# Block 0 of a convolution and two-layer kernel: its first layer from 12-bit operands, its staged words kept in g, five roundings of w_out moved behind it

## The chip, the cores and the metric

The kernel runs on one core of a Trainium2 chip. The metric is the time of one execution on the device, in microseconds, taken as the median of several runs. A core has TensorE (PE in the profile, with its weight loads as PEld), VectorE (DVE), ScalarE (ACT), GpSimd (POOL) and SyncE (SP), which issues most DMAs. Each engine works through its own queue of instructions in the order in which the program has them; semaphores join the queues.

## The reference

Eight sequences of 4096 tokens with 192 features go through a causal convolution of 7 taps, whose weights are a softmax shared by the 24 features of a head; then each token goes through two layers with a hard swish between them.

```python
w = softmax(weight)                         # 8 heads x 7 taps
out[b, s] = sum_k w[:, k] * x_pad[b, s + k]  # per head, 24 features each
h = x @ w_in                                # (32768, 192) @ (192, 2048)
g = h * clip(h + 3, 0, 6) / 6
return g @ w_out                            # (32768, 2048) @ (2048, 192)
```

w_in and w_out arrive as 64-bit floats. x, and the result, are 32-bit.

## The kernel before

Tokens are taken in 32 blocks of 1024, each block as two groups of 512 that lie in the two halves of the partitions. Features lie as 64 partitions by three thirds (K3 = 3). w_in's 2048 columns are 16 chunks of 128; a chunk index c runs from 0 to 7 and covers two of them, one for each half of the partitions. A first-layer unit (c, group) gives two PSUM banks: the group "own" multiplies y as it lies, the group "other" multiplies y with its two halves exchanged by DMA (`swap`). `relu` on ScalarE (L308) and `gate` on VectorE (L312) turn a unit's banks into its place in the tile g, which holds all of a block's hidden layer.

Blocks 1 to 31 use `first_layer` (L508): each operand is split into a high part of 12 bits (ScalarE multiplies by CUT and rounds, `high_of`, L480), a low part (the subtraction `low_of`, L483) and the full value. Three passes, high × high, low × high and full × low, are 18 matmuls for each unit, and PSUM is used as four slots of two banks. Their second layer (L593) is written out with due times. Block 0 is different: its first layer (`h_mm`, `half_mm`, L302) multiplies 32-bit operands, and its second layer `out_direct` (L347) runs three rounds over the eight chunks of w_out, four results side by side. w_out's chunk p is needed when a round comes to p.

The weights have no loading phase. Each of 16 units (eight of w_in, eight of w_out) goes through class `Rounding`, from 64-bit words to 32-bit floats: `load` (DMA on SP's queue, four units ahead), `split` (two instructions on VectorE, L177 and L181), `clamp` (three on ScalarE, L189, L192, L195), `join` (two on VectorE, L198 and L202, then a multiplication on POOL, L206). The order of all this is written by hand (`manual_schedule`): at the start the units 0 to 2 stand between the steps of block 0's convolution, of which TensorE takes one third (`pe_tap`, L794) after three matmuls on zeros (L802). In the loop over the 16 parts, ten of them (`slots`) carry the join of unit n, the clamp of n+1 and the split of n+2; three joins stand behind the loop.

```python
            def between():
                if more:
                    join(n)
                    clamp(n + 1)
            ...
            h_out(c, group, bs, (lambda: None) if first else between)
            if more:
                split(n + 2)
```

`prepare`, in the first round of `out_direct`, makes w_in's three parts for the later blocks from the finished w_in (`w_parts`: ScalarE L480 and L487, POOL L483), then block 1's convolution (L899) and its split. `begin_block_two`, in the third round, forms sums of w_out (L218, L565) and begins the next convolution.

Of the kernel before, what the change touches and what calls it, by code (L numbers as in the profile page):

```python
# [31 lines left out]
def kernel(  # L32
# [39 lines left out]
    start_pools, first_in = ExitStack(), ExitStack()  # L72
    stg = start_pools.enter_context(tc.tile_pool(name="stg", bufs=8))
    cnv = start_pools.enter_context(tc.tile_pool(name="cnv", bufs=4))
    fi = first_in.enter_context(tc.tile_pool(name="fi", bufs=1, side="right"))
# [40 lines left out]
    zeros = cnv.tile([P, N], F32, name="zeros", bufs=1)  # L116
    nc.vector.memset(zeros[:], 0.0)


    w_in = fi.tile([P, NP, K3, P], F32, name="w_in")  # L120


# [10 lines left out]
    def stage():  # L133
        return stg.tile([P, WS, 2], U32, name="stage")

    def load_w_in(j):
        st = stage()
        for half in range(2):
            nc.sync.dma_start(  # L139
                out=st[half * D2 : (half + 1) * D2].rearrange("p (s f) w -> p s (f w)", s=K3),  # L140
                in_=w_in_bits[j + half * NP].rearrange("p s f w -> p s (f w)"),
            )
        return st

    def load_w_out(j):
        st = stage()
        nc.sync.dma_start(
            out=st[:].rearrange("p (k d) w -> p k (d w)", k=2), in_=w_out_bits[:, j]
        )
        return st  # L150
# [7 lines left out]
    class Rounding:  # L158
# [13 lines left out]
        def split(self):  # L172
# [4 lines left out]
            nc.vector.tensor_scalar(  # L177
# [3 lines left out]
            nc.vector.tensor_scalar(  # L181
# [15 lines left out]
        def join(self):  # L197
            nc.vector.scalar_tensor_tensor(  # L198
                out=self.scale[:], in0=self.st[:, :, 1], scalar=0x80000000,
                in1=self.scale[:], op0=ALU.bitwise_and, op1=ALU.bitwise_or,  # L200
            )
            nc.vector.scalar_tensor_tensor(  # L202
                out=self.sig[:], in0=self.top[:], scalar=2.0**-20, in1=self.sig[:],
                op0=ALU.mult, op1=ALU.add,
            )
            nc.gpsimd.tensor_tensor(  # L206
                out=self.dst, in0=self.sig[:], in1=self.scale[:].bitcast(F32), op=ALU.mult
            )
    def w_in_unit(j):
        return Rounding(lambda: load_w_in(j), w_in[:, j].rearrange("p s f -> p (s f)"))  # L210

    def w_out_unit(j):
        dst = w_out[:, j, B11 : B22 + 1].rearrange("p b d -> p (b d)")
        return Rounding(lambda: load_w_out(j), dst)
# [29 lines left out]
    y_swapped = fi.tile([P, K3, N], F32, name="y_swapped")  # L244
    OWN, OTHER = 0, K3
# [29 lines left out]
    def swap_first(part):  # L275
        swap(y_swapped[:, part], y[:, part])

    g = cst.tile([P, NP, 2, G, N], F32, name="g")
# [6 lines left out]
    free_banks = list(range(2 * 4))  # L285

    def take():
        return free_banks.pop(0)

    def give(b):  # L290
        free_banks.append(b)

    def half_mm(k, b, w, third_of_y, start=False, stop=False, onto=False):

        r = slice(k * D2, (k + 1) * D2)  # L300
        src = y[r, third_of_y] if third_of_y < K3 else y_swapped[r, third_of_y - K3]
        nc.tensor.matmul(  # L302
            out=psum[:, b], lhsT=w[r], rhs=src, start=start, stop=stop,
            skip_group_check=onto,
        )
# [9 lines left out]

    def h_mm(c, group, bs, s, order=range(K3)):

        for k in range(2):
            half_mm(k, bs[k], w_in[:, c, s], group + s, s == order[0], s == order[-1])

    def g_of(c, group, k):

        return g[:, c, k, k if group == OWN else 1 - k]

    def h_out(c, group, bs, between):
        for k, b in enumerate(bs):
            relu(g_of(c, group, k), psum[:, b])
        between()
        for k, b in enumerate(bs):
            gate(g_of(c, group, k), psum[:, b])  # L330
            give(b)

# [44 lines left out]
    def out_direct(i, work):  # L383

        parts = [(k, q) for k in range(G) for q in range(G * NQ)]
        for r in range(0, len(parts), 4):
            b = take()
# [16 lines left out]
            give(b)  # L404
# [20 lines left out]

    def product(bank, j, n, q, ks=every, **tokens):
        x, w = prod[n]
        return mm(bank, j, S3 if n == 7 else x, w, q, ks, True, True, **tokens)

    def four(*parts):  # L430

        b = take()
        bank = psum[:, b]
        side_by_side(*[product(bank, j, n, q) for j, (n, q) in enumerate(parts)])
        return b, bank

    def three(n, n4, q4):
        return four(*[(n, q) for q in range(NQ)], (n4, q4))

    def by_quarters(n, q):  # L440

        b = take()
        bank = psum[:, b]
        w = NP // 4
        side_by_side(
            *[product(bank, j, n, q, range(j * w, (j + 1) * w)) for j in range(4)]
        )
        return b, bank
# [27 lines left out]
    def r32(ap):  # L476
        return ap.bitcast(F32R)

# [6 lines left out]
    def w_parts(high, low, full, w):  # L485
        high_of(high, w)
        nc.scalar.copy(out=r32(full), in_=w)  # L487
        low_of(low, w, high, nc.gpsimd)

    free_slots = list(range(4))  # L490
    y_own, y_other, pools, s1 = [], [None], [], []

    def swap_parts():
        y_other[0] = pools[0].tile([P, 2, K3, N], F32, name="y_other", tag="other")
        for n in range(2):
            swap(y_other[0][:, n], y_own[n])


    def first_layer(i, jobs):

        def unit(n):
            group, c = divmod(n, NP)
            slot = free_slots.pop(0)
            for m_, (wn, yn) in enumerate(PASSES):
                for s in range(K3):
                    for k in range(2):
                        r = slice(k * D2, (k + 1) * D2)
                        nc.tensor.matmul(  # L508
                            out=psum[:, 2 * slot + k], lhsT=r32(w_in_parts[wn][r, c, s]),
                            rhs=r32(y_other[0][r, yn, s] if group else y_own[yn][r, s]),  # L510
                            start=m_ == s == 0, stop=m_ == 2 and s == K3 - 1,
                            skip_group_check=True,
                        )
            both = psum[:, 2 * slot : 2 * slot + 2]
            to = g4[:, c, 1:3] if group else g4[:, c, 0::3]
# [263 lines left out]
    with tc.manual_schedule():  # L779
# [19 lines left out]
        b = take()  # L799
        for _ in range(3):  # L800

            nc.tensor.matmul(  # L802
                out=psum[:, b], lhsT=zeros[:, 0:P], rhs=zeros[:], start=True, stop=True
            )
        for k in range(KC):
# [3 lines left out]
        b1 = take()  # L809
        pe_tap(b1, 1, pe_taps, pe_taps)  # L810


        order = (pe_third, 0, 1)
        parts = [(c, group) for p in range(0, NP, 2) for group in (OWN, OTHER)
                 for c in (p, p + 1)]
        early = {}

        def begin(c, group):
            early[c, group] = take(), take()
            for s in order[:2]:  # L820
                h_mm(c, group, early[c, group], s, order)
# [3 lines left out]
        for k, u in enumerate(conv0[: per + 2 * pe_taps]):  # L825
# [3 lines left out]
            elif k == per - 3:  # L829
                join(0, more=False)  # L830
                split(1)
                nc.scalar.copy(out=y[:, pe_third], in_=psum[:, b])
                give(b)
                swap_first(thirds[pe_third])
                clamp(1)
            elif k in (per, per + 1):
                if k == per:
                    swap_first(thirds[0])
                    load(AHEAD)
                    begin(0, OWN)  # L840
# [8 lines left out]
        give(b1)  # L849
        swap_first(thirds[1])  # L850
# [5 lines left out]
        for c, group in ((0, OTHER), (1, OWN), (1, OTHER)):  # L856
            begin(c, group)
        for c, group in parts[: len(early)]:
            h_mm(c, group, early[c, group], order[2], order)

        slots = [0, 1, 3, 4, 6, 7, 9, 10, 12, 13]
        n = 3
        for slot, (c, group) in enumerate(parts):
            first = slot < len(early)
            if first:
                bs = early[c, group]
            else:
                bs = take(), take()
                for s in range(K3):
                    h_mm(c, group, bs, s)  # L870
            more = slot in slots

            def between():
# [3 lines left out]

            if slot == 6:
                x_tiles[1] = load_x(1)
            h_out(c, group, bs, (lambda: None) if first else between)  # L880
            if more:
                split(n + 2)
                if first:
                    between()
                n += 1
# [6 lines left out]
        late = ctx.enter_context(tc.tile_pool(name="late", bufs=1, reuse_waits="tile"))  # L892
        w_in_parts = [late.tile([P, NP, K3, P], F32, name=f"w_in{n}") for n in range(3)]
# [21 lines left out]
        def prepare():  # L915
            for n in range(0, NP, 4):
                r = slice(n, n + 4)
                w_parts(*[w[:, r] for w in w_in_parts], w_in[:, r])
            for job in conv_jobs(1):
                job()  # L920
            first_in.close()
            later = ctx.enter_context(tc.tile_pool(name="later", bufs=1, reuse_waits="tile"))
            y_own.extend(later.tile([P, K3, N], F32, name=f"y{n}") for n in range(2))
            pools.append(ctx.enter_context(tc.tile_pool(name="oth", bufs=1, reuse_waits="tile")))
# [69 lines left out]
```

## Time and profile before

| | |
|---|---|
| median of 3 runs | 2225.67 us (2225.53 to 2225.78) |
| the profiled execution | 2225.73 us, its span 2223.6 us |
| TensorE's share of the span | 100% (weight loads 69%) |
| VectorE, ScalarE, GpSimd | 81%, 42%, 37% |
| block 0's first layer, from and to | 17.3 to 58.5 us |
| block 0's second layer | 58.5 to 99.8 us |
| block 1's first layer | 99.9 to 132.7 us |

Times within the span are counted from its start. Each row of the timeline gives start, length, engine, line, operation, the tiles out and in, their shapes and how many instructions were merged. Instructions of one engine overlap a little, so the distance of two starts is shorter than the first one's length. The span ends about 2.1 us short of the measured time. A matmul of 32-bit operands shows as two records, one from 12-bit operands as one. Line numbers before the change are those of the kernel above; after it, `relu` is L299, `gate` L303, block 0's and all other first-layer matmuls L436 and `out_direct` L314.

### The profile page before, as it was taken

The numbers are of one execution on the slowest core, as the hardware profiler recorded it, in microseconds if no ns is written. First come the engines' busy times: TensorE is split into PE (matmuls) and PEld (weight loads), VectorE is DVE, ScalarE is ACT, GpSimd is POOL, SyncE is SP. The second block draws the span as 40 slices with busy tenths as digits, with TensorE's granted clock in tenths as the row PEclk, the third lists the DMA queues.
The fourth block names the chain that finished last, engine by engine and source line by source line (L and its number), as shares of the span: only waits on it lengthen the run. The fifth ranks groups of instructions, "written<-read, shape, count | busy, mean of one in ns | idle before, by whom it ended". The sixth has DMA issues, their size and how long they took to land.

```text
span 2223.6 us, 49133 instructions
## 1 busy us (share of the span) xinstructions
PE 2216.4 (100%) x21496; PEld 1536.0 (69%) x21496; DVE 1810.3 (81%) x1607; ACT 938.1 (42%) x1182; POOL 819.8 (37%) x692
## 2 busy tenths in 40 slices
PE   9999999999999999999999999999999999999999
PEld 5467776677766777766777667776677776677766
DVE  8788888887888888888888888888888888788866
ACT  7444443344433444334444334443344433344433
POOL 2434432344422444223443224442244432344322
PEclk9999999999999999999999999999999999999999
DMA  6233223333234342243322333323433224333232
GB/s 157 58 68 72 49 44 77 70 70 65 38 67 77 63 77 35 57 77 70 70 52 43 75 73 67 70 36 64 77 65 75 39 53 77 70 70 55 40 60 34
DMA packets 248613, 142.10 MB, mean 64 GB/s; under 512 B 207024, under 2 KB 212144, under 8 KB 248400
## 3 DMA queue, kind: packets, MB, share of 16 engines
q1 hardware_dynamic: 229912, 105.08, 23.3%
q0 software_dynamic: 17248, 33.64, 8.7%
q8 instruction: 168, 2.75, 0.5%
q10 hardware_dynamic: 1240, 0.27, 0.1%
q14 instruction: 45, 0.37, 0.1%
HBM read 31.72 MB, written 25.17 MB: 26 GB/s over the span
## 4 chain that ended last, share of the span: by engine, by line
PE 99%; DMA 0%; DVE 0%; SPq 0%; ACT 0%; issue 0%; DVEq 0%; ACTq 0%
PE psum L593 49%; PE psum L508 46%; PE psum L302 2%; PE psum L347 2%; DMA x<-in_x_dram 0%; SPq L106 0%; SPq L139 0%; DVE top L181 0%; PE psum L794 0%; DVE y L261 0%; DVE results L462 0%; SPq L95 0%; ACT y L808 0%; ACT scale L192 0%; ACT sig L195 0%
## 5 line engine op out<-in xcount | busy, mean ns | idle before, releaser
L593 PE MATMUL psum<-g,w_out 128*32 128x512 f32 (+1 forms) x6712 | 967.4, 552 | 0.0
L308 ACT ACTIVATE g<-psum,half 128x1024 f32<-128x1024 f32 (+1 forms) x528 | 574.2, 1092 | 487.8 <-PE psum L508 459.8
L312 DVE SCALAR_TENSOR_TENSOR g<-g,psum 128x1024 f32<-128x1024 f32 (+1 forms) x528 | 619.6, 1185 | 195.5 <-ACT g L308 195.1
L556 POOL TENSOR_TENSOR s<-g 128x256 f32<-128x256 f32 x248 | 267.0, 1077 | 1252.9 <-DVE g L312 877.3
L593 PEld LDWEIGHTS psum<-g,w_out 128*32 128x32 f32 x6712 | 371.8, 110 | 246.3 <-issue 126.9
L508 PE MATMUL psum<-y,w_in 64*128 64x512 f32 x4464 | 515.3, 388 | 0.0
L508 PE MATMUL psum<-y_other,w_in 64*128 64x512 f32 x4464 | 510.9, 386 | 0.0
L508 PEld LDWEIGHTS psum<-y,w_in 64*128 64x128 f32 x4464 | 415.8, 184 | 112.3 <-issue 26.0
L508 PEld LDWEIGHTS psum<-y_other,w_in 64*128 64x128 f32 x4464 | 418.1, 184 | 87.8
L593 PE MATMUL psum<-s,w_out 128*32 128x512 f32 (+1 forms) x3272 | 465.4, 570 | 0.0
L899 DVE SCALAR_TENSOR_TENSOR y<-x,c_sb,y 128x1536 f32<-128x1536 f32 x186 | 336.7, 1810 | 8.4 <-ACT y L897 7.2
L418 POOL TENSOR_TENSOR s<-g 128x1024 f32<-128x1024 f32 x93 | 297.8, 3203 | 25.0 <-DVE g L312 25.0
L593 PE MATMUL psum<-g,w_s 128*32 128x256 f32 x1240 | 282.8, 379 | 0.0
L593 PEld LDWEIGHTS psum<-s,w_out 128*32 128x32 f32 x3272 | 154.5, 110 | 80.2 <-issue 48.3
L593 PEld LDWEIGHTS psum<-g,w_s 128*32 128x32 f32 x1240 | 136.4, 110 | 67.7
L418 DVE TENSOR_TENSOR s<-g 128x2048 f32<-128x2048 f32 (+1 forms) x93 | 177.2, 1933 | 1.1
L593 PE MATMUL psum<-s,w_s 128*32 128x256 f32 x744 | 170.7, 379 | 0.0
L556 DVE TENSOR_TENSOR g<-g 128x1024 f32<-128x1024 f32 x124 | 151.7, 1224 | 6.0 <-DVE g L556 0.9
L418 DVE TENSOR_TENSOR g<-g 128x2048 f32<-128x2048 f32 x62 | 139.1, 2284 | 0.0
L462 DVE TENSOR_TENSOR p<-psum,p 32x256 f32<-32x256 f32 (+1 forms) x93 | 47.7, 513 | 95.5 <-PE psum L593 94.1
L462 DVE TENSOR_TENSOR results<-psum,results 32x256 f32<-32x256 f32 (+3 forms) x128 | 69.3, 541 | 51.1 <-issue 47.6
L590 ACT COPY psum<-psum 32x512 f32<-32x512 f32 x93 | 51.3, 551 | 135.3 <-PE psum L593 135.3
(87 smaller groups left out, 1152.4 us busy)
## 6 DMA issues: line engine op xcount, KB each, us to landing
y_other<-y SPq DMA_DIRECT2D x124, 384.0 KB, 5.0
g<-g POOLq DMA_DIRECT2D x62, 512.0 KB, 5.0
out_dram<-results SPq DMA_DIRECT2D x378, 64.0 KB, 2.0
x<-in_x_dram SPq DMA_DIRECT2D x53, 388.5 KB, 7.0
stage<-in_moe_w_in_dram SPq DMA_DIRECT2D x16, 192.0 KB, 4.6
stage<-in_moe_w_out_dram SPq DMA_DIRECT2D x8, 384.0 KB, 7.3
x<-in_x_dram SPq DMA_DIRECT2D x7, 384.0 KB, 6.5
x<-in_x_dram POOLq DMA_DIRECT2D x2, 388.5 KB, 5.4
```

Of the source, the lines that this page charges most:

```text
L302: nc.tensor.matmul(out=psum[:, b], lhsT=w[r], rhs=src, start=start, stop=stop, skip_group_check=onto,)
L308: nc.scalar.activation(r6, h, ACT.Relu, bias=half[:], scale=1.0 / 6.0)
L312: nc.vector.scalar_tensor_tensor(out=g_, in0=g_, scalar=1.0, in1=h, op0=ALU.min, op1=ALU.mult)
L347: lambda p=p: nc.tensor.matmul(out=bank[j * QS : (j + 1) * QS, tokens], lhsT=w_out[:, p, w, cols], rhs=x[:, p, tokens], start=(first and p ...
L418: engine.tensor_tensor(out=o[:, r], in0=a[:, r], in1=b[:, r], op=op)
L462: nc.vector.tensor_tensor(out=out, in0=x, in1=y, op=op)
L508: nc.tensor.matmul(out=psum[:, 2 * slot + k], lhsT=r32(w_in_parts[wn][r, c, s]), rhs=r32(y_other[0][r, yn, s] if group else y_own[yn][r, s ...
L556: engine.tensor_tensor(out=o, in0=p, in1=q, op=op)
L590: streams[3].append((t - 0.5, lambda: fn(*args, **kw)))
L593: nc.tensor.matmul(out=out, lhsT=w, rhs=x, start=start, stop=True, tile_position=(0, j * QS), skip_group_check=True,)
L899: jobs.append(lambda k=k: nc.vector.scalar_tensor_tensor(out=y[:], in0=x[:, :, k : k + N], scalar=c_sb[:, k : k + 1], in1=y[:], op0=ALU.mu ...
```

## The change

Block 0's first layer is done as in the later blocks, from 12-bit operands in three passes, with the same function `products`. For this, each w_in unit is rounded straight into its three parts within `join`: POOL's multiplication now writes into `sig`; ScalarE makes the high part from it; POOL copies it into the full part and subtracts for the low part. `w_parts` in `prepare` goes. The convolution result of block 0 is split into high and low third by third (`parts_of`), and both parts are swapped, so that 12 swap DMAs stand where 6 stood. The words of w_in's eight units are staged in the upper half of g, with w_out's in four buffers of `stg` (eight shared ones before); the buffers of `cnv` go from four to three. The PSUM banks become four slots, and relu and gate take both banks of a unit at once. The order of parts is now c by c, own then other. Six of the units are joined within the loop over c (c = 0 to 4 and 7, in the group "own"), ten before; seven joins, w_out's units 1 to 7, stand behind the loop, three before. An `engine` argument of `split` is not used by any call.

```diff
-    stg = start_pools.enter_context(tc.tile_pool(name="stg", bufs=8))
-    cnv = start_pools.enter_context(tc.tile_pool(name="cnv", bufs=4))
+    stg = start_pools.enter_context(tc.tile_pool(name="stg", bufs=4))
+    cnv = start_pools.enter_context(tc.tile_pool(name="cnv", bufs=3))
...
+    early_stages = [
+        g[:, c].rearrange("p h k n -> p (h k n)").bitcast(U32)[:, t : t + 2 * WS]
+        .rearrange("p (f w) -> p f w", w=2)
+        for c in range(NP - 4, NP) for t in (0, 2 * WS)
+    ]
...
+            dst = self.sig[:] if in_parts else self.dst[0]
             nc.gpsimd.tensor_tensor(
-                out=self.dst, in0=self.sig[:], in1=self.scale[:].bitcast(F32), op=ALU.mult
-            )
+                out=dst, in0=self.sig[:], in1=self.scale[:].bitcast(F32), op=ALU.mult
+            )
+            if in_parts:
+                high, low, full = self.dst
+                nc.scalar.mul(r32(high), dst, CUT)
+                nc.gpsimd.tensor_copy(out=r32(full), in_=dst)
+                nc.gpsimd.tensor_tensor(out=r32(low), in0=dst, in1=high, op=ALU.subtract)
...
+    def products(n, slot, s, steps=range(3), begin=False, end=False):
+        group, c = divmod(n, NP)
+        for m_ in steps:
+            wn, yn = PASSES[m_]
+            for k in range(2):
+                r = slice(k * D2, (k + 1) * D2)
+                nc.tensor.matmul(
+                    out=psum[:, 2 * slot + k], lhsT=r32(w_in_parts[wn][r, c, s]),
+                    rhs=r32(y_other[r, yn, s] if group else y_own[yn][r, s]),
+                    start=begin and m_ == 0, stop=end and m_ == 2, skip_group_check=True,
+                )
...
+        def parts_of(s, of):
+            high, low = (part[:, thirds[s]] for part in y_own)
+            high_of(high, of)
+            low_of(low, of, high, nc.vector)
+            swap_parts(thirds[s])
...
-                nc.scalar.copy(out=y[:, pe_third], in_=psum[:, b])
-                give(b)
-                swap_first(thirds[pe_third])
+                parts_of(pe_third, psum[:, b : b + 1])
...
-        slots = [0, 1, 3, 4, 6, 7, 9, 10, 12, 13]
+        slots = [0, 1, 2, 3, 4, 7]
         n = 3
...
+        for c in range(NP):
+            if c == 3:
+                x_tiles[1] = load_x(1)
+            for group in range(2):
...
+                to, both = places(k, slot)
+                relu(to, both)
+                more = group == 0 and c in slots
                 if more:
                     join(n)
                     clamp(n + 1)
...
+                gate(to, both)
+                free_slots.append(slot)
+                if more:
+                    split(n + 2)
+                    n += 1
         while n < len(units):
             join(n)
             clamp(n + 1)
             split(n + 2)
             n += 1
...
         def prepare():
-            for n in range(0, NP, 4):
-                r = slice(n, n + 4)
-                w_parts(*[w[:, r] for w in w_in_parts], w_in[:, r])
             for job in conv_jobs(1):
                 job()
```

More of the change, by code (lines that the diff above doesn't have):

```diff
@@ L71 @@
     ps = ctx.enter_context(tc.tile_pool(name="ps", bufs=1, space=bass.MemoryType.PSUM))
-    start_pools, first_in = ExitStack(), ExitStack()
-    stg = start_pools.enter_context(tc.tile_pool(name="stg", bufs=8))
-    cnv = start_pools.enter_context(tc.tile_pool(name="cnv", bufs=4))
-    fi = first_in.enter_context(tc.tile_pool(name="fi", bufs=1, side="right"))
+    start_pools = ExitStack()
+    stg = start_pools.enter_context(tc.tile_pool(name="stg", bufs=4))
+    cnv = start_pools.enter_context(tc.tile_pool(name="cnv", bufs=3))
     def x_source(i):
@@ L115 @@
     diag = cnv.tile([P, KC, P], F32, name="diag", bufs=1)
-    zeros = cnv.tile([P, N], F32, name="zeros", bufs=1)
-    nc.vector.memset(zeros[:], 0.0)
-    w_in = fi.tile([P, NP, K3, P], F32, name="w_in")
+    g = cst.tile([P, NP, 2, G, N], F32, name="g")
+    zeros = g[:, 0, 0, 0]
+    nc.vector.memset(zeros, 0.0)
+    w_in_parts = [cst.tile([P, NP, K3, P], F32, name=f"w_in{n}") for n in range(3)]
+    y_own = [cst.tile([P, K3, N], F32, name=f"y{n}") for n in range(2)]
+    y_other = cst.tile([P, 2, K3, N], F32, name="y_other")
     w_out = cst.tile([P, NP, 7, DH], F32, name="w_out")
@@ L131 @@
     assert 2 * D == WS
-    def stage():
-        return stg.tile([P, WS, 2], U32, name="stage")
+    early_stages = [
[3 more added lines that the diff above has]
+    ]
     def load_w_in(j):
-        st = stage()
+        st = early_stages[j]
         for half in range(2):
@@ L145, in load_w_out @@
     def load_w_out(j):
-        st = stage()
+        st = stg.tile([P, WS, 2], U32, name="stage")
         nc.sync.dma_start(
@@ L149, in load_w_out @@
         )
-        return st
+        return st[:]
     EXP1 = 1 << 20
@@ L170, in load, with split @@
             self.st = self.load_words()
-        def split(self):
+        def split(self, engine=nc.vector):
             high = self.st[:, :, 1]
@@ L176, in split @@
             self.sig = cnv.tile([P, WS], F32, name="sig")
-            nc.vector.tensor_scalar(
+            engine.tensor_scalar(
                 out=self.scale[:], in0=high, scalar1=0x7FF00000, scalar2=None,
@@ L180, in split @@
             )
-            nc.vector.tensor_scalar(
+            engine.tensor_scalar(
                 out=self.top[:], in0=high, scalar1=0xFFFFF, scalar2=0x100000,
@@ L201, in join @@
             )
+            in_parts = len(self.dst) > 1
             nc.vector.scalar_tensor_tensor(
@@ L205, in join, with r32 @@
             )
+            dst = self.sig[:] if in_parts else self.dst[0]
             nc.gpsimd.tensor_tensor(
-                out=self.dst, in0=self.sig[:], in1=self.scale[:].bitcast(F32), op=ALU.mult
+                out=dst, in0=self.sig[:], in1=self.scale[:].bitcast(F32), op=ALU.mult
             )
+            if in_parts:
[3 more added lines that the diff above has]
+                nc.gpsimd.tensor_tensor(out=r32(low), in0=dst, in1=high, op=ALU.subtract)
+    def r32(ap):
+        return ap.bitcast(F32R)
     def w_in_unit(j):
-        return Rounding(lambda: load_w_in(j), w_in[:, j].rearrange("p s f -> p (s f)"))
+        dst = [w[:, j].rearrange("p s f -> p (s f)") for w in w_in_parts]
+        return Rounding(lambda: load_w_in(j), dst)
     def w_out_unit(j):
         dst = w_out[:, j, B11 : B22 + 1].rearrange("p b d -> p (b d)")
-        return Rounding(lambda: load_w_out(j), dst)
+        return Rounding(lambda: load_w_out(j), [dst])
     def w_sums(sums):
@@ L243 @@
     y = ys.tile([P, K3, N], F32, name="y")
-    y_swapped = fi.tile([P, K3, N], F32, name="y_swapped")
-    OWN, OTHER = 0, K3
+    OWN, OTHER = range(2)
     def conv_units(i, parts, cuts=1):
@@ L273, in swap @@
         nc.sync.dma_start(out=to[0:D2], in_=part[D2:P])
-    def swap_first(part):
-        swap(y_swapped[:, part], y[:, part])
-    g = cst.tile([P, NP, 2, G, N], F32, name="g")
     g4 = g[:].rearrange("p c h k n -> p c (h k) n")
@@ L284 @@
     psum = ps.tile([P, 2 * 4, N], F32, name="psum")
[L285 to L304, printed above, removed]
-        )
+    free_slots = list(range(4))
     def relu(r6, h):
@@ L314, in gate @@
         )
[L316 to L330, printed above, removed]
-            give(b)
     def dff_half(k):
@@ L386, in out_direct @@
         for r in range(0, len(parts), 4):
-            b = take()
+            b = 2 * free_slots[r // 4]
             bank = psum[:, b]
@@ L403, in out_direct @@
             nc.vector.transpose(out=xt[:], in_=bank)
-            give(b)
             for j, (k, q) in enumerate(parts[r : r + 4]):
@@ L424 @@
     }
[L426 to L448, printed above, removed]
     def rows(q):
@@ L472 @@
     m = slice(0, DH)
-    def r32(ap):
-        return ap.bitcast(F32R)
     def high_of(out, x):
@@ L483, in low_of, with swap_parts, places @@
         engine.tensor_tensor(out=r32(out), in0=x, in1=high, op=ALU.subtract)
[L485 to L494, printed above, removed]
-        for n in range(2):
-            swap(y_other[0][:, n], y_own[n])
+    s1 = []
+    def swap_parts(thirds=slice(0, K3)):
+        for n in range(2):
+            swap(y_other[:, n, thirds], y_own[n][:, thirds])
+    def products(n, slot, s, steps=range(3), begin=False, end=False):
[9 more added lines that the diff above has]
+                )
+    def places(n, slot):
+        group, c = divmod(n, NP)
+        return g4[:, c, 1:3] if group else g4[:, c, 0::3], psum[:, 2 * slot : 2 * slot + 2]
     def first_layer(i, jobs):
         def unit(n):
-            group, c = divmod(n, NP)
             slot = free_slots.pop(0)
-            for m_, (wn, yn) in enumerate(PASSES):
+            for m_ in range(3):
                 for s in range(K3):
[L506 to L515, printed above, removed]
+                    products(n, slot, s, (m_,), s == 0, s == K3 - 1)
+            to, both = places(n, slot)
             relu(to, both)
@@ L797, in pe_tap @@
             )
-        b = take()
+        b, b1 = (2 * free_slots[-1] + k for k in range(2))
         for _ in range(3):
             nc.tensor.matmul(
-                out=psum[:, b], lhsT=zeros[:, 0:P], rhs=zeros[:], start=True, stop=True
+                out=psum[:, b], lhsT=zeros[:, 0:P], rhs=zeros, start=True, stop=True
             )
@@ L808, with begin @@
         nc.scalar.mul(y[:, 1], x0[:, 1, 0:N], c_sb[:, 0:1])
-        b1 = take()
         pe_tap(b1, 1, pe_taps, pe_taps)
         order = (pe_third, 0, 1)
-        parts = [(c, group) for p in range(0, NP, 2) for group in (OWN, OTHER)
-                 for c in (p, p + 1)]
         early = {}
-        def begin(c, group):
-            early[c, group] = take(), take()
+        def begin(n):
+            early[n] = free_slots.pop(0)
             for s in order[:2]:
-                h_mm(c, group, early[c, group], s, order)
+                products(n, early[n], s, begin=s == order[0])
+        def parts_of(s, of):
[3 more added lines that the diff above has]
+            swap_parts(thirds[s])
         conv0 = conv_units(0, thirds[:pe_third], 2)
@@ L831 @@
                 split(1)
-                nc.scalar.copy(out=y[:, pe_third], in_=psum[:, b])
-                give(b)
-                swap_first(thirds[pe_third])
+                parts_of(pe_third, psum[:, b : b + 1])
                 clamp(1)
@@ L837 @@
                 if k == per:
-                    swap_first(thirds[0])
+                    parts_of(0, y[:, thirds[0]])
                     load(AHEAD)
-                    begin(0, OWN)
+                    begin(0)
                     pe_tap(b1, 1, pe_taps + 1, pe_taps)
@@ L848 @@
         add(y[:, 1], psum[:, b1], y[:, 1])
-        give(b1)
-        swap_first(thirds[1])
+        parts_of(1, y[:, thirds[1]])
         join(2)
@@ L854 @@
         split(4)
[L856 to L859, printed above, removed]
-        slots = [0, 1, 3, 4, 6, 7, 9, 10, 12, 13]
-        n = 3
[L863 to L873, printed above, removed]
+        for n in (1, NP):
+            begin(n)
+        for n in early:
+            products(n, early[n], order[2], end=True)
+        slots = [0, 1, 2, 3, 4, 7]
+        n = 3
+        for c in range(NP):
+            if c == 3:
+                x_tiles[1] = load_x(1)
+            for group in range(2):
+                k = group * NP + c
+                if k in early:
+                    slot = early[k]
+                else:
+                    slot = free_slots.pop(0)
+                    for m_ in range(3):
+                        for s in range(K3):
+                            products(k, slot, s, (m_,), s == 0, s == K3 - 1)
+                to, both = places(k, slot)
+                relu(to, both)
+                more = group == 0 and c in slots
                 if more:
@@ L876, in between @@
                     clamp(n + 1)
[L878 to L885, printed above, removed]
+                gate(to, both)
[3 more added lines that the diff above has]
+                    n += 1
         while n < len(units):
@@ L891 @@
         start_pools.close()
-        late = ctx.enter_context(tc.tile_pool(name="late", bufs=1, reuse_waits="tile"))
-        w_in_parts = [late.tile([P, NP, K3, P], F32, name=f"w_in{n}") for n in range(3)]
         def conv_jobs(i):
@@ L915, in prepare @@
         def prepare():
-            for n in range(0, NP, 4):
-                r = slice(n, n + 4)
-                w_parts(*[w[:, r] for w in w_in_parts], w_in[:, r])
             for job in conv_jobs(1):
                 job()
[L921 to L924, printed above, removed]
             x_tiles[2] = load_x(2, nc.gpsimd)
```

## The prediction

> **What bounds the kernel now.** I read the chain of waits first, in order of time. Columns: start, length, what.
>
> ```profile
> 17.28 41.27 PE psum L302 x184
> 58.56 41.34 PE psum L347 x384
> 99.89 32.87 PE psum L508 x288
> ```
>
> From 17 us on TensorE is the chain, without a break: block 0's first layer (L302), its second (L347), then block 1. The page gives PE 99% of the whole chain. So only what block 0 makes of TensorE's time counts, and block 1's first matmul at 99.89 us is the mark; a shift of it goes to the end unchanged. 288 matmuls with 12-bit operands take 32.87 us in block 1, the full-precision ones 41.27 us.
>
> Next, busy time by stage (PE, PEld, DVE, ACT, POOL):
>
> ```profile
> 17.00:58.50 41.50, 41.50 (x187) 26.00 (x187) 39.65 (x83) 37.12 (x66) 12.51 (x12) 1.00 0.54 143
> 58.50:72.30 13.80, 13.80 (x133) 4.23 (x136) 7.83 (x13) 12.34 (x15) 8.52 (x5) 1.00 0.01 1
> ```
>
> TensorE is only just the bound: in 41.5 us VectorE is busy for 39.65 and ScalarE for 37.12, with the gates, the relus and ten roundings. A saving on TensorE alone cannot be cashed in. The second layer's first round (13.8 us) has slack on VectorE.
>
> Then the timeline, for the price of one rounding on ScalarE (clamp: 25.36 to 27.12, 1.76 us; two relus follow, 1.14 us to the next clamp), and of the larger relu and gate of later blocks (in brackets, idle time before and what ended it):
>
> ```profile
> 25.36 0.61 ACT L189 ACTIVATE sig<-scale,bias_e 128x384 f32<-128x384 uint32 x1
> 26.01 0.62 ACT L192 ACTIVATE scale<-sig,bias_e 128x384 uint32<-128x384 f32 x1
> 26.66 0.57 ACT L195 ACTIVATE sig<-stage 128x384 f32<-128x384 uint32 x1
> 27.12 1.25 ACT L308 ACTIVATE g<-psum,half 128x512 f32<-128x512 f32 x2
> ...
> 102.21 1.12 ACT L308 ACTIVATE g<-psum,half 128x1024 f32<-128x1024 f32 x1 [8.42 <-PE psum L508]
> ...
> 103.36 1.22 DVE L312 SCALAR_TENSOR_TENSOR g<-g,psum 128x1024 f32<-128x1024 f32 x1
> ```
>
> Last, the timeline of the tail, where roundings stand with no gates between them:
>
> ```profile
> 60.95 0.55 DVE L198 SCALAR_TENSOR_TENSOR scale<-stage,scale 128x384 uint32<-128x384 uint32 x1
> ...
> 61.42 0.54 DVE L202 SCALAR_TENSOR_TENSOR sig<-top,sig 128x384 f32<-128x384 uint32 x1
> ...
> 61.89 0.35 DVE L177 TENSOR_SCALAR scale<-stage 128x384 uint32<-128x384 uint32 x1
> ...
> 62.04 1.06 POOL L206 TENSOR_TENSOR w_out<-sig,scale 128x384 f32<-128x384 f32 x1 [4.46 <-DVE sig L202]
> 62.16 1.16 DVE L181 TENSOR_SCALAR top<-stage 128x384 uint32<-128x384 uint32 x1
> ...
> 63.24 0.55 DVE L198 SCALAR_TENSOR_TENSOR scale<-stage,scale 128x384 uint32<-128x384 uint32 x1
> ```
>
> Join plus split take 2.29 us (60.95 to 63.24) though the four instructions alone make about 1.5: L181 takes 1.16 instead of 0.35 us because the multiplication on POOL runs. Gates, which read PSUM, kept 0.6 us each beside such a multiplication.
>
> **What TensorE saves.** 41.27 − 32.87 = 8.4 us, if fed.
>
> **The start, to the first relu (24.23 us before).** Added on VectorE up to join(2), which started at 21.15: three subtractions for y's low part at 0.61 (pitch of the 128x512 addition at 20.54), 1.8; waits for ScalarE's high parts. The first waits behind POOL's multiplication of unit 0 (ends 13.64), w_in's high part and y's high part, about 14.75, where VectorE was free at 13.78: 1.0. The second waits behind clamp(1), 0.7; the third for its own high part, 0.6. POOL's copy and subtraction of unit 1 each hold VectorE as in the fence above, 1.0 together (unit 0's run while VectorE waits anyway). Sum 5.1. After join(2) ScalarE now has the multiplication to wait for (1.04) and the high part to make (0.47) before clamp(3) and the relu, 0.3 of which replaces split's own 0.3: +1.25. First relu: 24.23 + 5.1 + 1.25 = 30.6.
>
> POOL's copy is in no row. POOL's rows bound it: the two-input multiplication of this shape at its longest, 1.32 at 16.85, from above, the 128x128 memset, 0.24, from below; I take 0.65, about the middle of 0.24 and the usual 1.0. It stands on the path twice, in units 1 and 2, so the bounds move the end by −0.8 and +1.3. It is new work, so it gains nothing. The subtraction is 3.49/4 = 0.87, from the 128x1536 one at 67.05. Six further swaps put 3.6 us on SP's queue (0.6 each), ahead of the loads of units 4 to 6. Unit 4's lands at about 24 (issued near 19, 4.6 us to landing) and is split at about 28; without those 4 us of cover the start would slip by the rest. The stages in g cost nothing: units 0 to 7 are joined two chunks or more before their place in g is written.
>
> **The loop.** Here ScalarE gets a new wait. Its queue runs relu(c−1, group 1), relu(c, group 0), high part of unit n, clamp(n+1), relu(c, group 1). The high part needs POOL's multiplication, which needs join(n), which stands on VectorE behind gate(c−1, group 1), and that gate needs the relu that ScalarE did at the start. So nothing overlaps: relu 1.12 + gate 1.15 to the next start + join 0.47 + 0.55 + multiplication 1.0 + high part 0.47 + clamp 1.76, and some 0.05 for each of the handovers = 6.7 us for each c with a w_in unit, where TensorE needs 2 × 2.05 = 4.1. Behind the waiting high part stand the clamp and the next relu; behind that relu, its gate, the PSUM slot and TensorE. In the before kernel nothing of ScalarE's queue waits for POOL here: that is the difference.
> Times: relu(0, group 0) 30.6; relu(0, 1) 4.1 later, 34.7; four cycles for c = 1 to 4, 34.7 + 26.8 = 61.5. Then no unit stands in c = 5 and 6. gate(4, 1) ends at 63.9 and frees the slot for the fourteenth unit; three units of 2.05 follow: the first layer ends at 70.1 instead of 58.5. Lost so far: 11.6 us.
>
> **The tail.** join(8), w_out's first unit, sits in c = 7; its multiplication ends near 70.4, so round 0 begins at once. Joins 9 to 15 (seven, three before) come behind the last gate: relu(7, 1) waits for clamp(9) until 71.0, its gate ends at 73.3, join(9) and its multiplication end at 75.3. Then 2.29 each, six more: 89.05; the last multiplication finds the next convolution step on VectorE (1.81 us, two SBUF inputs), about +0.9: 90.0. Chunk 7's eight matmuls (1.7 us) end round 0 at 91.7, where it ended at 72.3. Loads of units 12 to 15 reuse buffers, but each has two units (4.6 us) until its split and an idle DMA (share 0.01 in that window): nothing. Rounds 1 and 2 take 27.5 us as now. The conversions taken out of prepare (four of 1.4 us on ScalarE, two of 3.5 on POOL) ran under the second layer and were worth nothing; their absence lets the convolution, 13 us, the split of y, w_sums and conv(2) end about 113, before round 2 does. Block 1 starts at 91.7 + 27.5 = 119.2.
>
> **Sum.** 119.2 − 99.8 = +19.4 us. On the profiled execution, 2225.73 (span 2223.6 and 2.1 around it; the median 2225.67 is the same), 2245.1 us.
>
> [...]
>
> **Rivals.**
> A, faster: TensorE still sets the pace, 8.4 us are gained, 2217.3. For it: 32.87 us in block 1, and PE 99% of the chain. It needs a cycle of at most 4.1 us per c, and the in-order sum is 6.7. Chance 4%; by this mechanism, partly cashed in, also no change, 2%.
> B, slower but less: the cycle shrinks to ScalarE's own work, 2 × 1.04 + 0.47 + 1.76 = 4.3 us, if VectorE runs far enough ahead. Four cycles would then end at 51.9, and TensorE's own 16 × 2.05 from its first full unit near 29 would set the end of the layer, 62, 8 us before 70.1; the tail's part stays: 2237. Against it: join stands behind the gate in VectorE's queue. 7%.
> C, TensorE runs cold. The row: the warm-up's six records take 4.99 us, 0.83 each, the next sixteen 0.44, though the granted clock reads 1.00.
>
> ```profile
> 1.49 4.99 PE L802 MATMUL psum<-zeros 128*128 128x512 f32 x6 [1.49 <-DVE half L239]
> 6.32 7.07 PE L794 MATMUL psum<-x,diag 128*128 128x512 f32 x16
> ```
>
> In the loop TensorE would idle 2.6 us of every 6.7. If such gaps halve its speed, a chunk takes 8.2 instead of 6.7 us four times, and the last three units 4.1 each for a while: +6 to +10, 2251 to 2255. [...] 12%.
> D, no change because the change does not do what it says: the built order shows the f32r matmuls and the seven late joins, 1%.
>
> **How the numbers follow.** Forecast 74%, C 12, B 7, A 4 and 2, D 1. Range 2239 to 2255: the forecast with the copy's bounds (−0.8, +1.3), 5 us below for the 5.1 and handovers of the start if VectorE hides them, and C above; B, A and D are left out, 14 in 100. A measurement here can tell 0.2%, 4.5 us. Faster by more: 0.04; within: 0.03; slower: 0.93.
>
> **What would show it.** In the profile after: first relu near 30.6; ScalarE idle about 2 us ahead of each high part with POOL named as releaser; relus of group 1 6.7 us apart for c = 1 to 4; L314 from about 70; round 0 over 20 us long with TensorE waiting for POOL; block 1 at 119. It is wrong if ScalarE is never idle there, or block 1 starts before 110.

## The result, and the profile after

The changed kernel takes 2245.3 us (2245.11 to 2246.72, 6 runs), the kernel before 2225.6 beside it (2225.12 to 2225.92, 6 runs): the ratio is 1.009, with a 95% interval of 1.0077 to 1.0103. That is 19.7 us more, where 19.4 was forecast. The profiled execution took 2245.11 us, its span 2243.0.

The chain of waits, in order of time (start, length, what), is read first again. One turn of block 0's first layer, the last unit of the first round of its second layer, and the beginning of block 1:

```profile
41.33 1.01 ACT g L299
42.37 1.07 DVE g L303
43.51 0.55 DVE scale L202
...
44.61 1.02 POOL sig L212
45.65 0.52 ACT w_in L217
...
47.91 1.01 ACT g L299
...
87.14 2.50 POOL w_out L212
89.69 29.39 PE psum L314 x272
119.08 1.12 PE psum L436 x7
```

Before, TensorE alone stood in this stretch. Now there is no TensorE between 41.33 and 47.91: relu, gate, join, POOL's product, ScalarE's high part, the clamp of the next unit and the next relu follow each other on three engines, 6.58 us for one c. TensorE comes back into the chain for good only at 89.69, after the last product of w_out. Block 1 begins at 119.08 instead of 99.89: +19.2 of the 19.4 by which the two profiled executions differ. From there the two chains have the same rows (block 1's first layer 32.86 and 32.87 us).

The rows left out of the turn are the rest of join (L207) and the clamp. ScalarE's timeline (in brackets the idle time before, and what ended it) shows the wait itself:

```profile
41.24 2.10 ACT L299 ACTIVATE g<-psum,half 128x1024 f32<-128x1024 f32 x2
45.65 0.52 ACT L217 ACTIVATE w_in<-sig 128x384 fp32r<-128x384 f32 x1 [2.31 <-POOL sig L212]
```

ScalarE stands idle 2.3 us before the high part, and behind that wait stand a clamp and a relu that have nothing to do with it. In the kernel before, the list of ScalarE's waits from 24 to 60 us is empty. The waits of ScalarE and TensorE, added up (us in total, times, longest us), give both halves of the loss, first ScalarE's from 24 to 92 us, then TensorE's to 120 us:

```profile
ACT w_in L217 <- POOL sig L212: 12.8, 6, 2.8
...
PE psum L436 <- DVE g L303: 9.3, 6, 2.2
PE psum L314 <- POOL w_out L212: 5.3, 5, 2.9
```

TensorE's timeline, from the last unit of the first layer into the tail:

```profile
67.61 2.20 PE L436 MATMUL psum<-y_other,w_in 64*128 64x512 f32 x18
70.24 1.92 PE L314 MATMUL psum<-g,w_out 128*32 128x512 f32 x16 [0.42 <-POOL w_out L212]
75.06 8.79 PE L314 MATMUL psum<-g,w_out 128*32 128x512 f32 x64 [2.90 <-POOL w_out L212]
...
89.69 29.39 PE L314 MATMUL psum<-g,w_out 128*32 128x512 f32 x272 [1.07 <-POOL w_out L212]
```

The first layer ended at 69.8 (58.5 before). Round 0 then goes at the pace of the roundings: one chunk of w_out for each product on POOL, until 89.7.

### The profile page after: what moved, and what is told of

The parts are those of the page before. It is cut to its first block, busy times and chain, and to the rows that moved or that the text cites. A ratio compares the mean times of both kernels' runs of the same rounds, so it can differ in the third digit from the quotient of the medians.

```text
span 2243.0 us, 49324 instructions
## 1 busy us (share of the span) xinstructions
PE 2216.2 (99%) x21592; PEld 1537.8 (69%) x21592; DVE 1816.9 (81%) x1594; ACT 935.8 (42%) x1172; POOL 830.4 (37%) x706
## 4 chain that ended last, share of the span: by engine, by line
PE 96%; DVE 2%; ACT 1%; POOL 0%; issue 0%; DMA 0%; ACTq 0%; DVEq 0%; POOLq 0%
PE psum L532 49%; PE psum L436 46%; PE psum L314 1%; DVE y L276 0%; DVE g L303 0%; ACT g L299 0%; DVE sig L207 0%; DVE scale L202 0%; POOL sig L212 0%; DVE top L185 0%; DMA x<-in_x_dram 0%; POOL w_out L212 0%; DVE scale L181 0%; ACT w_in L217 0%; ACT scale L196 0%
## 5 line engine op out<-in xcount | busy, mean ns | idle before, releaser
L303 DVE SCALAR_TENSOR_TENSOR g<-g,psum 128x1024 f32<-128x1024 f32 x512 | 618.8, 1218 | 206.5 <-ACT g L299 206.3
L299 ACT ACTIVATE g<-psum,half 128x1024 f32<-128x1024 f32 x512 | 571.5, 1118 | 495.0 <-PE psum L436 466.9
L436 PE MATMUL psum<-y_other,w_in 64*128 64x512 f32 x4608 | 530.5, 387 | 10.5 <-DVE g L303 8.7
L436 PE MATMUL psum<-y,w_in 64*128 64x512 f32 x4608 | 536.1, 389 | 4.2 <-ACT y L419 1.9
L436 PEld LDWEIGHTS psum<-y,w_in 64*128 64x128 f32 x4608 | 429.9, 185 | 124.1 <-issue 26.0
L436 PEld LDWEIGHTS psum<-y_other,w_in 64*128 64x128 f32 x4608 | 431.9, 184 | 103.4 <-DVE g L303 10.9
```

The costliest lines, as they stand in the source:

```text
L299: nc.scalar.activation(r6, h, ACT.Relu, bias=half[:], scale=1.0 / 6.0)
L303: nc.vector.scalar_tensor_tensor(out=g_, in0=g_, scalar=1.0, in1=h, op0=ALU.min, op1=ALU.mult)
L436: nc.tensor.matmul(out=psum[:, 2 * slot + k], lhsT=r32(w_in_parts[wn][r, c, s]), rhs=r32(y_other[r, yn, s] if group else y_own[yn][r, s]), ...
```

## The experiments

The theory under test is the prediction's; where an expectation numbers its theories, it is the first. The time is lost in the loop because ScalarE's in-order queue waits for POOL, and in the tail because seven w_out units now come behind the loop. The saving on TensorE is eaten by the later start. The rivals put the loss on TensorE (its work, or its clock) or on VectorE's and POOL's amount of work. Every ratio is against the kernel before, with its 95% interval.

**The three parts issued later.** The high part, POOL's copy and the subtraction are taken out of `join` and issued after the next part's relu. The amount of work is the same.

```diff
-            if in_parts:
+        def make_parts(self):
+            if len(self.dst) > 1:
...
                 relu(to, both)
+                if group and waiting:
+                    waiting.pop().make_parts()
                 if more:
-                    join(n)
+                    join(n, parts=False)
+                    waiting.append(units[n])
                     clamp(n + 1)
```

> The only edit: within the loop, the three instructions that make a w_in unit's parts (high part on ScalarE, copy and subtraction on POOL) are issued after the next part's relu, not in join. Theory 1 (ScalarE's queue stands behind POOL's multiplication): the cycle falls from the 6.56 us of the changed kernel (relus at 41.24 and 47.80) to ScalarE's own work, 2 x 1.04 + 0.47 + 1.76 = 4.3; four cycles save 9, the part c = 0 about 1 more. First layer ends near 60 instead of 69.8, block 1 begins near 109, time 2234 to 2237. [...] Theory 3 (TensorE at half rate after its gaps): at most the 1 us that the slow unit at 43.65 cost, 2244.

Measured: 2234.43 us (2234.32 to 2234.61), ratio 1.0039 (1.0025 to 1.0054): 10.9 us of the 19.7 are back. ScalarE's timeline no longer has a gap before the high part, and TensorE's units stand back to back (the third fence is the chain of waits, in which TensorE alone stands from 35.89 to 55.1):

```profile
37.65 1.10 ACT L301 ACTIVATE g<-psum,half 128x1024 f32<-128x1024 f32 x1
38.65 0.51 ACT L219 ACTIVATE w_in<-sig 128x384 fp32r<-128x384 f32 x1
...
41.81 1.10 ACT L301 ACTIVATE g<-psum,half 128x1024 f32<-128x1024 f32 x1
```

```profile
38.14 2.35 PE L438 MATMUL psum<-y,w_in 64*128 64x512 f32 x18
40.33 2.26 PE L438 MATMUL psum<-y_other,w_in 64*128 64x512 f32 x18
...
79.02 26.39 PE L316 MATMUL psum<-g,w_out 128*32 128x512 f32 x244 [1.07 <-POOL w_out L212]
```

```profile
35.89 19.20 PE psum L438 x162
```

The turn, 37.65 to 41.81, is now 4.16 us, about TensorE's own two units. The first layer ends at 59.1. The tail has the waits of the changed kernel, 10.7 us earlier (its last at 79.02, 89.69 there): it wasn't touched. So it is the order of issue, not the amount of work, that costs the 10.9 us.

**The parts issued after the clamp.** A half step: the clamp of the next unit no longer stands behind the wait, group 1's relu still does.

```diff
-                    join(n)
+                    join(n, parts=False)
                     clamp(n + 1)
+                    units[n].make_parts()
```

> The changed kernel, with the three instructions that make a unit's parts issued behind clamp(n+1), still ahead of the relu of group 1. Theory 1: the clamp (1.76 us) then runs while POOL multiplies, the rest of the chain stays: cycle 6.58 - 1.76 = 4.8; four cycles and c = 0 save 8 to 9, 2236.5 to 2238, that is 2 to 3 us more than with the parts behind the relu (2234.4). If it were the multiplication alone that costs (1.02 us) the order against the clamp would not matter: 2245.

Measured: 2237.52 us (2237.43 to 2237.72), ratio 1.0053 (1.0036 to 1.007). ScalarE's timeline keeps a small gap:

```profile
43.33 0.53 ACT L219 ACTIVATE w_in<-sig 128x384 fp32r<-128x384 f32 x1 [0.59 <-POOL sig L212]
43.77 2.10 ACT L301 ACTIVATE g<-psum,half 128x1024 f32<-128x1024 f32 x2
...
48.63 2.10 ACT L301 ACTIVATE g<-psum,half 128x1024 f32<-128x1024 f32 x2
```

From one such pair of relus to the next the turn is 4.86 us, 1.72 less than 6.58: the clamp, 1.76 as the prediction priced it, now runs while VectorE joins and POOL multiplies. The first layer ends at 62.3.

**Ten roundings in the loop.** The units are joined at the ten part numbers that the kernel before uses; the parts stay inside `join`.

```diff
-        slots = [0, 1, 2, 3, 4, 7]
+        slots = [0, 1, 3, 4, 6, 7, 9, 10, 12, 13]
...
-                more = group == 0 and c in slots
+                more = 2 * c + group in slots
```

> The only edit: ten units are joined within the loop, at the part numbers that the kernel before used (0, 1, 3, 4, 6, 7, 9, 10, 12, 13); three joins stand behind it. Theory 1: the five waits of w_in's units stay, each chain 6.6 us, w_out's units cost ScalarE no wait; so the first layer ends about where it did (70 to 72), and four joins of 2.29 us, 9.2, leave the tail, of which some 6 are gained, since round 0 needs 13.8 us by itself after 70.2: 2238 to 2241. Theory 2: VectorE is full, so four units of 1.48 us in the loop push the first layer by 6, and nothing is gained: 2244 to 2247.

Measured: 2237.98 us (2237.89 to 2238.08), ratio 1.0055 (1.004 to 1.007): 7.3 us are back, at the lower edge of the first theory's range. TensorE's timeline:

```profile
70.44 12.22 PE L314 MATMUL psum<-g,w_out 128*32 128x512 f32 x112
82.82 29.39 PE L314 MATMUL psum<-g,w_out 128*32 128x512 f32 x272 [0.15 <-POOL w_out L212]
```

The first layer ends at 70.5, no earlier than in the changed kernel, so nothing of the loop's loss is won back. The reason is not quite the one expected: ScalarE's waits for POOL shrink a little (9.6 us in all for 12.8), but the clamps of w_out's units now stand in the loop, and from 53.7 to 72.8 us ScalarE's clamps and relus are the chain, one behind the other. Round 0 takes 12.4 us instead of 19.5 up to its last chunk. This is the price of putting four more w_out units behind the loop (the title counts five; it is seven joins there for three).

**Both edits.** The parts are issued after every next relu, with ten roundings in the loop, at places chosen for this order and not those of the last run.

```diff
-        slots = [0, 1, 2, 3, 4, 7]
+        slots = [0, 1, 2, 4, 6, 8, 9, 11, 12, 14]
+        waiting = []
...
                 relu(to, both)
+                if waiting:
+                    waiting.pop().make_parts()
```

> Both edits at once (parts issued after the next relu; ten units in the loop, at parts 0, 1, 2, 4, 6, 8, 9, 11, 12, 14). If the two losses are separate and only waits, they add: 10 + 6, 2229. If VectorE becomes the bound once the waits are gone, its work from the first gate on counts: 16 x 1.14 + 10 x 1.48 = 33 us from 30.7, so the first layer ends near 64 and round 0 about 15 later: block 1 near 105, 2231 to 2233. In both cases still slower than the kernel before, by 3 or by 7 us.

Measured: 2230.46 us (2230.26 to 2230.83, 10 runs), ratio 1.0022 (1.0012 to 1.0031). That lies between the two expectations, 2229 and 2231 to 2233. The gain of 14.8 is 3.4 short of 10.9 + 7.3, in part perhaps because the ten places differ. By stage (us; then busy time and number of instructions of PE, PEld, DVE, ACT, POOL; granted clock, DMA share, GB/s):

```profile
31.00:72.80 41.80, 39.52 (x333) 26.46 (x333) 40.98 (x64) 40.00 (x59) 20.63 (x22) 0.96 0.43 109
```

VectorE is busy for 40.98 of 41.8 us and ScalarE for 40.0, and in the chain of waits no TensorE stands between 26.7 and 75.5 us: with the waits gone, the amount of work on these two is the next limit. The kernel is the fastest here that keeps the change and all of its rounding, and it is still 4.8 us behind the kernel before.

**The w_out product on VectorE.** Only the products of w_out leave POOL.

```diff
-            nc.gpsimd.tensor_tensor(
+            engine = nc.gpsimd if in_parts else nc.vector
+            engine.tensor_tensor(
```

> The only edit: the last multiplication of a w_out unit runs on VectorE instead of POOL. If the tail's 2.29 us for each unit come from POOL's multiplication holding VectorE's next instruction (1.16 instead of 0.35), the pace becomes 0.94 + 0.47 + 0.54 = 1.95, six times 0.34 = 2.0 are saved, and the last product (2.50 us beside the convolution's first step) takes about 0.5, another 1.3 to 1.9: 2241 to 2242.5. Rival: the tail is bound by ScalarE's clamp (1.76, and 0.40 of idle ahead of each): then three more products of 0.47 on VectorE cost or gain nothing, 2244 to 2247.

Measured: 2242.67 us (2242.6 to 2242.7), ratio 1.0076 (1.0061 to 1.0091): 2.6 us are back, a little less than the first theory expected. After the first wait of 2.86 us TensorE runs through:

```profile
74.66 41.47 PE L315 MATMUL psum<-g,w_out 128*32 128x512 f32 x368 [2.86 <-DVE w_out L213]
```

So the product's place on POOL makes 2.6 us of the tail's cost. The first wait, for the joins behind the last gate, is about the same as before the edit (2.90). The row's 368 matmuls take 41.47 us, some 1.7 more than at the pace of the changed kernel's last row of L314 (272 in 29.39, which gives 39.8). How much earlier block 1 would have begun without these 1.7 us is not shown, since TensorE would then have come sooner to products that may not have been done.

**TensorE given more work in the loop.** In the units of c = 1 to 4 that are not begun early the first pass is issued twice: six matmuls more in each of seven units (the expectation says eight and adds up seven).

```diff
-                    for m_ in range(3):
+                    for m_ in (0, 0, 1, 2) if 0 < c < 5 else range(3):
```

> The changed kernel with more work for TensorE: in the eight units of c = 1 to 4 (those not begun early) the first pass of six matmuls is issued twice, the second starting the sum anew, 0.69 us more for each unit of 2.05. Theory 1 (ScalarE's queue sets the cycle): TensorE idles 2.2 us of every 6.6, so 2 x 0.69 for each c fit in, and the time stays within 0.5 us of 2245.3; by filling the gaps it might even keep the granted clock at 1.00. If TensorE's work, at full or at half rate, were on the path in the loop: 7 units x 0.69 = +4.8, 2250.

Measured: 2246.82 us (2245.42 to 2247.11, 4 runs), ratio 1.0093 (1.0078 to 1.0109). That is 0.1 to 1.8 above the changed kernel, outside the 0.5 that the first theory allowed and far from the 4.8 us that were added to TensorE. In TensorE's timeline the turn stays at 6.6 us, and the extra comes at one place behind the seven units (the second fence is the stage, columns as above):

```profile
63.65 3.91 PE L436 MATMUL psum<-y_other,w_in 64*128 64x512 f32 x18 [2.16 <-DVE g L303]
```

```profile
64.00:66.00 2.00, 2.00 (x12) 1.59 (x10) 2.00 (x3) 1.35 (x2) 0.00 (x0) 0.50 0.00 0
```

The unit at 63.65 has no extra matmuls, yet takes 3.91 us instead of 2.2: its granted clock was 0.50. It is one of the last three units and stands in the chain of waits, so most of these 1.7 us count. That the half clock makes the difference is shown for the two executions with a trace alone, 2247.11 here and 2245.11 of the changed kernel: one execution here took 2245.42, one of the changed kernel 2246.72, and neither has a trace. Lowest against lowest, and highest against highest, the added 4.8 us move the time by no more than 0.4: TensorE's work in the loop is off the path.

**Rounding left out, in both kernels.** From unit 3 on the weights are copied, not rounded (`copy_words` in place of split, clamp and join); in the changed kernel the three parts are still made.

```diff
-        units[n].join()
+        units[n].join() if n < 3 else units[n].copy_words()
```

> The kernel before with the rounding left out from unit 3 on: split, clamp and join become one copy of the upper words, so w_in and w_out hold other numbers (matmuls take the same time). TensorE was the bound from 17 us on, so nothing or little is gained: 2224.5 to 2225.7. If VectorE or ScalarE were the bound (39.65 and 37.12 of 41.5 us busy), several us would go.

> The changed kernel with the same part left out (units 3 to 15 are copied, w_in's three parts are still made). If the 12-bit matmuls save TensorE's 8.4 us once they are fed, only the later start (first relu 30.7 instead of 24.2) stands against it: three units are done near 32.5, thirteen more at 2.05 end the first layer at 59, and block 1 begins near 100 to 101: 2224 to 2228, level with the kernel before. If the loss were in the 12-bit path itself (smaller matmuls, swaps, half rate), it would stay above 2235.

Measured: the kernel before 2224.43 us (2224.37 to 2224.5), ratio 0.9994 (0.9985 to 1.0003); the changed kernel 2225.54 us (2225.31 to 2225.74), ratio 0.9999 (0.999 to 1.0009). Without the roundings the first gets 1.3 us shorter, the second 19.8, and the second is still 1.1 us behind the first. The other numbers in the weights do not move the matmuls: the 384 of the second layer take 41.41 us with them, 41.34 with the rounded ones. The kernel before hides the roundings under TensorE nearly whole; in the changed one they are the whole loss. TensorE's timelines, of the kernel before and then of the changed one:

```profile
57.43 41.41 PE L351 MATMUL psum<-g,w_out 128*32 128x512 f32 x384
```

```profile
54.85 2.21 PE L449 MATMUL psum<-y_other,w_in 64*128 64x512 f32 x18
...
99.42 16.61 PE L449 MATMUL psum<-y,w_in 64*128 64x512 f32 x144
```

Fed without a break, the layer from 12-bit operands ends at 57.0, against 57.4 for the 32-bit one without rounding. All but 0.4 of the 8.4 us that it saves on TensorE go into its later start: TensorE runs without a break from 22.9 us on, from 17.1 in the kernel before. Its matmuls are slow there at first (the 12 from 25.23 to 27.80 come 0.21 us apart, those of the later units 0.11), which hardly counts: the unit at 29.49 needs the last swap, for which the same unit of the changed kernel, its granted clock back at 0.99 from 20.9 to 22.0, waits 1.73 us and starts at 29.37. This bounds the change: even with every rounding after the first three units turned into a copy it was not faster.

## Why the prediction was right

**The start.** The first relu starts at 30.66 (30.6 forecast), join(2) at 26.32 (21.15 + 5.1 = 26.25). VectorE's timeline has the three waits, priced at 1.0, 0.7 and 0.6, at 0.99, 0.69 and 0.70. The rows are ScalarE's first relu, then VectorE's first wait and six steps of the convolution, then the same steps in the kernel before:

```profile
30.66 1.11 ACT L299 ACTIVATE g<-psum,half 128x1024 f32<-128x1024 f32 x1
```

```profile
14.59 0.69 DVE L422 TENSOR_TENSOR y<-psum,y 128x512 fp32r<-128x512 f32 x1 [0.99 <-ACT y L419]
...
20.03 4.18 DVE L276 SCALAR_TENSOR_TENSOR y<-x,c_sb,y 128x256 f32<-128x256 f32 x6
```

```profile
17.23 3.20 DVE L261 SCALAR_TENSOR_TENSOR y<-x,c_sb,y 128x256 f32<-128x256 f32 x6
```

The hold-up by POOL (1.0) is in the convolution: the six steps take 4.18 us where they took 3.20. POOL's two unknown prices were each off, one up and one down. The copy, taken as 0.65, is 0.50 to 0.61; the subtraction, taken as 0.87, is 0.99 to 1.14. They nearly cancel, which is luck. One copy and subtraction of the loop (POOL's timeline):

```profile
45.68 0.61 POOL L218 CAST w_in<-sig 128x384 fp32r<-128x384 f32 x1
46.26 1.11 POOL L219 TENSOR_TENSOR w_in<-sig,w_in 128x384 fp32r<-128x384 f32 x1
```

**The loop.** The wait is where it was put, 2.3 us with POOL as releaser (about 2 forecast). The turn is 6.58 us for 6.7: the terms together were a little cheaper. Over four turns this makes the layer end at 69.8 for 70.1. The 4.1 us up to the second relu, for which the prediction shows no row, are 3.98, and ScalarE's wait is in them too (0.71), with the high part and the clamp. That the wait is the cause, and not the amount of work, is shown by the two edits of order, which take 7.8 and 10.9 us back with the same work.

**The tail.** The first late product ends at 75.0 (75.3), the last at 89.6 (90.0). The six steps of 2.29 and the 0.9 for the last product come out in the sum, though not in their parts (POOL's timeline):

```profile
85.39 1.25 POOL L212 TENSOR_TENSOR w_out<-sig,scale 128x384 f32<-128x384 f32 x1 [1.24 <-DVE sig L207]
87.13 2.50 POOL L212 TENSOR_TENSOR w_out<-sig,scale 128x384 f32<-128x384 f32 x1 [0.49 <-DVE sig L207]
```

No split stands between the last two joins, so the last product starts 1.74 us behind the one before it, not 2.29. It then takes 2.50 us beside the next convolution's steps on VectorE, where beside a split one took 1.04 (w_out's second unit at 73.96). Together that is −0.55 + 1.46, about the +0.9 of the prediction, an estimate for which no row stood: the collision was foreseen, that its size fits is luck.

**The sum.** Block 1 at 119.08 for 119.2, the time 2245.3 for 2245.1. The mechanism was right at each step; an agreement to 0.2 us is better than the terms, of which several are off by 0.1 to 1.5 us.

**The rivals.** A fell: TensorE waits 9.3 us for gates, and 4.8 us more work on it left the turn as it was. B fell for this order of issue. Its mechanism, a turn of ScalarE's own work, came about with the parts issued later (4.16 us for its 4.3), so it needed another order, not a faster VectorE. That its price, 2237, is near the 2237.5 of the clamp alone moved ahead says nothing: the turn is 4.86 us there. C's mechanism did occur, after gaps of 1.3 to 2.9 us (the last section has the rows), but cost nothing measurable in the changed kernel's profiled execution. The slow unit at 43.65 took 3.29 us inside a turn in which TensorE had 2.2 us to spare, and round 0's slow stretch, at 75.7, was caught up by 84.2, where TensorE waits for POOL again. The 6 to 10 us were too high, since they assumed slow units in every turn; where a slow stretch did fall on the path, with the first pass issued twice, it cost 1.7 us. D fell: the matmuls from 12-bit operands and seven products behind the loop are in the trace.

**Still open.** How the 4.8 us that remain with both edits divide between the later start and VectorE's and ScalarE's added work wasn't tried. The changed kernel's execution at 2246.72 has no trace.

## What to carry to other kernels

Before a step that needs another engine is put into an in-order queue, ask what stands behind it: here a 0.52 us instruction that waited 2.3 us delayed a clamp and a relu with no tie to it, and set TensorE's pace. Issuing the same work one relu later gave back 10.9 us. And a bound that is only just the bound (41.5 us of TensorE over 39.7 of VectorE) was not lowered by work that loads the runners-up; leave the work out on both sides, as in the last experiment, to see whether there was anything to win.

## What the runs showed of the hardware

The granted clock of TensorE fell to 0.50 for about 3.4 us at a time, three times in block 0 of the changed kernel: from 17.5, 44.8 and 75.5. In the kernel before it was 1.00 in every half microsecond from 0 to 130. Two of the three, by stage (columns as above):

```profile
44.70:48.10 3.40, 3.40 (x20) 2.63 (x18) 1.80 (x3) 2.39 (x5) 2.60 (x3) 0.52 0.01 2
48.10:49.00 0.90, 0.90 (x10) 0.77 (x8) 0.05 (x1) 0.90 (x2) 0.00 (x0) 0.93 0.00 0
...
75.70:78.90 3.20, 3.20 (x20) 0.59 (x13) 3.20 (x7) 2.31 (x5) 1.43 (x2) 0.50 0.55 169
```

The three follow gaps on TensorE of 1.3, 2.2 and 2.9 us, and each begins about 0.3 to 1.2 us after work has resumed. Other gaps of 2.2 us, before 56.8 and 63.4, were followed by none; with the pass issued twice the one before 63.65 was. So a slow stretch can follow a gap of 1.3 us and be absent after one of 2.2: which gap has one cannot be read from its length.

Read in steps of 0.1 us, the three last 3.4 to 3.5 us, and their onsets lie 27.3 and 30.7 us apart, near eight and nine times the length of one (27.2 and 30.6 for 3.4 us); three onsets are too few to read a rule from. In the 3.4 us ahead of the onsets TensorE was busy for 46%, 35% and 15%. That share does not separate the cases either: it was 35% from 60.0 to 63.4 and 37% from 53.4 to 56.8, and no slow stretch followed. So the condition stays open.
